# Attention numerators with tokens on partitions: q's exponentials become the stationary operand, the division happens on PSUM, and a TensorE transpose brings the result to x

## The chip, the cores and the metric

The kernel runs on one core of a Trainium2 chip. The metric is the device time of one execution in microseconds (us). The kernel before takes 989.12 us (median of three runs, 987.18 to 989.40). The execution that was profiled took 986.97 us, of which the profile's span is 984.9 us.

## The reference, cut to what matters

Linear attention with an exponential feature map, then two MLPs, one after the other:

```python
def phi(x):                                   # q, k, v: (4, 8, 576, 64) f32
    proj = einsum('bhsd,df->bhsf', x, w_phi)  # 128 features
    proj = proj - max(abs(proj), axis=-1)
    return concatenate([exp(proj), exp(-proj)], axis=-1)
q_p, k_p = phi(q), phi(k)
kv  = einsum('bhsf,bhsd->bhfd', k_p, v)
z   = sum(k_p, axis=2)
num = einsum('bhsf,bhfd->bhsd', q_p, kv)
den = einsum('bhsf,bhf->bhs', q_p, z)[..., None] + 1e-06
x   = (num / den) -> (2304 tokens, 512)
x   = elu(x @ w1_in) @ w1_out                 # 512 -> 2048 -> 512
out = h * clip(h + 3, 0, 6) / 6 @ w2_out      # h = x @ w2_in
```

The four MLP weights come as 64-bit floats. The kernel turns them into 32-bit floats with integer operations on the chip.

## The kernel before, in words

**Units.** The attention part is cut into 8 units. A unit is two heads of two batches, with 576 tokens each, laid as 9 tiles of 128 rows (64 tokens of one batch and 64 of the other). For each unit:

- `proj` (L316): TensorE projects k and q into four PSUM banks of ring "p".
- `peak` (L326) and `shift` (L340): VectorE takes the largest absolute value per row from PSUM and subtracts it. A unit has 8 such pairs 512 wide and 2 pairs 256 wide.
- `k_exp` (L349, L356): ScalarE makes k's exponentials of both signs.
- `kv` (L378): TensorE sums k's exponentials times [v, 1] into two banks, with 64 rows by 64 columns of the array in each matmul. Four places of the array are used in turn.
- `stat` (L393, L397): ScalarE copies these sums to SBUF (tile st). The sum z is repeated over the 64 columns that hold no values, so that the stationary operand is 128 columns wide.
- `q_tr`, `q_tr8` (L402, L408): TensorE transposes q's shifted projections into a bank of ring "t" (two banks). `q_exp` (L415, L424): ScalarE makes q's exponentials (tile e, features on partitions).
- `num` (L436): with st stationary (128 by 128) and e moving (256 or 320 tokens), 16 matmuls per unit make numerators on 64 partitions and the denominator, repeated, on the other 64. An f32 matmul leaves two records in the trace.
- `num_out` (L451, L455): ScalarE copies both to SBUF, with epsilon added to the denominators.
- `den`, `recip`, `recip_rows` (L460, L466, L474): VectorE transposes blocks of 32 by 32 so that each denominator is taken once, inverts, and transposes back. This happens four times per unit.
- `scale` (L483): GpSimd multiplies and writes x, with features on partitions, as the MLPs read it.

**Weights.** Each of the 64 weight tiles is converted by eight VectorE instructions (`begin` L681, `ts` L689, `into_b` L693) and then `end`, `w_hi`, `w_lo` on GpSimd (L698, L720, L726). A weight is held as a high and a low part, and so is x (`x_hi` on ScalarE L732, `x_lo` on VectorE L737).

**MLPs.** `hid` (L752) and `outp` (L813) each multiply three pairs of parts. Weights go in groups of four hidden tiles over all five blocks of tokens. The first block (512 tokens of batch 0) needs units 0 to 3 only, so its `hid` can start before the last unit is done.

**Order.** Nothing is ordered by hand. Each step has an engine, a planned duration, what it waits for, the buffers it takes and a rank. `in_order` plans all steps on all engines and the instructions are issued in the planned order, so every engine runs its own list strictly in turn. Ranks come from the unit's number times `PERIOD`, the length of the chain behind the step, and a table `BIAS` by kind of step. `W_LEAD` and `W_BIAS` rank the weight conversions.

Of the kernel before, what the change touches and what calls it, by code (L numbers as in the profile page):

```python
# [29 lines left out]
}  # L30
KVT = 0.118
W_LEAD, W_BIAS = 21.4, 113.0
# [19 lines left out]
WINDOW = 0.2  # L52
# [94 lines left out]
def attention_then_two_mlps(  # L147
# [82 lines left out]
    eps_c = bpool.tile([128, 1], F32, name="eps_c")  # L230
    nc.gpsimd.memset(eps_c, EPS)
# [7 lines left out]
    for i in range(2):  # L239
        t = apool.tile([128, R, 2, D + 1], F32, name=f"vb{i}")  # L240
        nc.gpsimd.memset(t[:, :, 0, D:D + 1], 1.0)
        nc.gpsimd.memset(t[:, :, 1, 0:1], 1.0)
        vb.append(t)
# [3 lines left out]
        "st0": 2, "st1": 2, "nsd": NSB, "t1": 1, "rr": 2, "rb": 2,  # L247
# [3 lines left out]
    MU = {}  # L251
    last = {}

    def unit(u):
# [12 lines left out]
        raw, P, M, SH, KP, acc, E, ST, NS, RB = ({} for _ in range(10))  # L267
# [10 lines left out]
        def load_v():  # L278
            src = v[u].rearrange("p (r h d) -> p r h d", r=R, h=2)
            for h in range(2):  # L280
                nc.sync.dma_start(out=vb[u % 2][:, :, h, h:h + D], in_=src[:, :, h])
# [102 lines left out]
        def stat_at(h):  # L384

            return (slice(0, 65), slice(64, 65), slice(65, 128)) if h == 0 else (
                slice(63, 128), slice(63, 64), slice(0, 63)
            )

        def stat(h):  # L390
            st = ST[h] = bpool.tile([128, 4, 128], F32, tag=f"st{h}", name="st", bufs=2)
            for bb in range(2):
                nc.scalar.copy(  # L393
                    out=st.rearrange("p (e b) d -> p e b d", e=2)[:, :, bb, stat_at(h)[0]], in_=acc[bb][:, h]
                )
            _, z, c = stat_at(h)
            nc.scalar.copy(out=st[:, :, c], in_=st[:, :, z].to_broadcast([128, 4, 63]))  # L397
# [13 lines left out]
        def q_exp(h, c):  # L411
            e = E[h, c] = bpool.tile([128, 2, 2, 4 + c, 64], F32, tag="e", name="e", bufs=EB)
            ps = P.pop(("q", h, c)).rearrange("p (r b t) -> p r b t", r=4, b=2)
            for half in range(2):
                nc.scalar.activation(  # L415
                    out=e[:, half, :, 0:4, :].rearrange("p b r t -> p r b t"), in_=ps, func=AF.Exp,
                    scale=1.0 if half == 0 else -1.0,
                )

        def q_exp8():  # L420
            ps = P.pop(("q", 8))
            for h in range(2):
                for half in range(2):
                    nc.scalar.activation(  # L424
                        out=E[h, 1][:, half, :, 4, :],
                        in_=ps[:, h * 128:(h + 1) * 128].rearrange("p (b t) -> p b t", b=2),
# [3 lines left out]
        def num(h, c, bb):  # L430
            e = E[h, c].rearrange("p e b r t -> p (e b r t)")
            n = 64 * (4 + c)
            ps = bank("t")
            for half in range(2):
                o = (half * 2 + bb) * n
                nc.tensor.matmul(  # L436
                    out=ps[:, :n], lhsT=ST[h][:, half * 2 + bb, :], rhs=e[:, o:o + n],
                    start=(half == 0), stop=(half == 1),
                )
            P["n", h, c, bb] = ps  # L440

        def num_out(h, c, bb):
            n = 64 * (4 + c)
            ps = P.pop(("n", h, c, bb))
            if (c, bb) not in NS:
                NS[c, bb] = tuple(
                    bpool.tile([128, 320], F32, tag="n" + s_, name="n" + s_, bufs=NSB) for s_ in "sd"
                )
# [565 lines left out]
```

## Time and profile before

| | before |
|---|---|
| median of three runs | 989.12 us (987.18 to 989.40) |
| the profiled execution | 986.97 us, span 984.9 us |
| TensorE (PE) busy | 966.0 us, 98% |
| VectorE (DVE) busy | 743.8 us, 76% |
| ScalarE (ACT) busy | 422.6 us, 43% |
| GpSimd (POOL) busy | 276.9 us, 28% |

The shares are means over two very different stages: the attention part, up to about 180 us, and the MLPs behind it. They have to be read apart. A busy PE is not PE at its peak: the ends of matmuls are modelled, and neighbours overlap.

### The profile page before, as it was taken

Reading aid. Unit: us, or ns where it says so; the run is one execution under the profiler, and the core shown is the slowest. Engines: PE = TensorE matmul, PEld = TensorE weight load, DVE = VectorE, ACT = ScalarE, POOL = GpSimd, SP = SyncE. Lnnn points to the kernel's source line nnn. Section 1 sums busy time; section 2 is a strip of 40 time slices with the busy share of each in tenths; the row PEclk is TensorE's granted clock in tenths of the full one; section 3 lists DMA queues with packets and bytes.
Section 4 is the critical chain, followed back from the end, with each engine's and each line's share of the span. In section 5 each row is a group of like instructions: output and inputs, shape, how many; then the busy total and the mean of one; then the engine's idle time right before and its main releaser. Section 6 shows DMA issues by size and latency. Waiting matters only on the chain.

```text
span 984.9 us, 17242 instructions
## 1 busy us (share of the span) xinstructions
PE 966.0 (98%) x7040; PEld 803.2 (82%) x7040; DVE 743.8 (76%) x1222; ACT 422.6 (43%) x831; POOL 276.9 (28%) x256
## 2 busy tenths in 40 slices
PE   8999999999999999999999999999999999999998
PEld 7777777788888888888887888888888888888887
DVE  5999999999858956895698958955986599643333
ACT  4888788864353333333344443333222222222222
POOL 0122323334234213421355363313321333130000
PEclk9999999999999999999999999999999999999999
DMA  7343321012202110211011201220122012001111
GB/s 210 107 133 107 96 79 38 23 44 65 84 2 65 55 53 1 65 52 56 1 44 43 65 22 44 65 65 1 44 65 65 1 43 65 22 1 43 43 43 64
DMA packets 33310, 53.66 MB, mean 54 GB/s; under 512 B 20304, under 2 KB 20432, under 8 KB 33232
## 3 DMA queue, kind: packets, MB, share of 16 engines
q1 hardware_dynamic: 33232, 52.57, 17.6%
q8 instruction: 55, 0.90, 0.4%
q14 instruction: 23, 0.19, 0.1%
HBM read 47.84 MB, written 4.72 MB: 53 GB/s over the span
## 4 chain that ended last, share of the span: by engine, by line
PE 81%; DVE 14%; ACT 4%; issue 1%; DVEq 0%; POOL 0%; ACTq 0%; POOLq 0%
PE ps_p L752 39%; PE ps_a L813 20%; PE ps_t L813 18%; DVE mx L326 3%; DVE shq L340 2%; PE ps_p L316 1%; DVE shk L340 1%; DVE w_b L693 1%; DVE rb L474 1%; DVE t L460 1%; DVE w_a L689 1%; DVE gl L794 1%; PE ps_t L436 1%; ACT kp L349 1%; ACT e L415 1%
## 5 line engine op out<-in xcount | busy, mean ns | idle before, releaser
L779 DVE SCALAR_TENSOR_TENSOR g<-e,ps_p 128x512 f32<-128x512 f32 (+1 forms) x160 | 101.1, 632 | 161.6 <-ACT e L768 105.9
L752 PE MATMUL ps_p<-xh,w_l 128*128 128x512 f32 (+1 forms) x512 | 185.6, 362 | 0.0
L752 PE MATMUL ps_p<-xl,w_h 128*128 128x512 f32 (+1 forms) x512 | 185.6, 362 | 0.0
L752 PE MATMUL ps_p<-xh,w_h 128*128 128x512 f32 (+1 forms) x512 | 185.5, 362 | 0.0
L698 POOL TENSOR_TENSOR w_b<-w_b,w 128x512 int32<-128x512 int32 x64 | 91.4, 1428 | 303.3 <-DVE w L689 303.3
L794 DVE TENSOR_TENSOR gl<-g,gh 128x512 fp32r<-128x512 f32 (+1 forms) x160 | 123.6, 773 | 47.9 <-ACT gh L787 43.7
L768 ACT ACTIVATE e<-ps_p,half_c 128x512 f32<-128x512 f32 (+1 forms) x80 | 51.7, 646 | 224.0 <-PE ps_p L752 224.0
L787 ACT CAST gh<-g 128x512 fp32r<-128x512 f32 (+1 forms) x160 | 92.6, 578 | 119.3 <-DVE g L779 119.2
L765 ACT ACTIVATE e<-ps_p 128x512 f32<-128x512 f32 (+1 forms) x80 | 44.4, 555 | 168.6 <-PE ps_p L752 168.6
L752 PEld LDWEIGHTS ps_p<-xh,w_h 128*128 128x128 f32 x512 | 96.6, 189 | 15.9
L752 PEld LDWEIGHTS ps_p<-xl,w_h 128*128 128x128 f32 x512 | 96.6, 189 | 15.9
L752 PEld LDWEIGHTS ps_p<-xh,w_l 128*128 128x128 f32 x512 | 96.5, 189 | 15.0
L689 DVE TENSOR_SCALAR w_a<-w_a 128x512 int32<-128x512 int32 x128 | 104.1, 813 | 1.4
L693 DVE SCALAR_TENSOR_TENSOR w_b<-w,w_b 128x512 int32<-128x512 int32 x128 | 89.6, 700 | 2.4
L726 POOL TENSOR_TENSOR w_l<-w_b,w_h 128x512 fp32r<-128x512 f32 x64 | 86.1, 1345 | 5.3
L720 POOL TENSOR_SCALAR w_h<-w_b 128x512 fp32r<-128x512 f32 x64 | 46.5, 726 | 139.4 <-PE ps_a L813 74.9
L436 PE MATMUL ps_t<-e,st 128*128 128x256 f32 (+1 forms) x256 | 70.4, 418 | 3.9 <-ACT st L397 2.8
L483 POOL TENSOR_TENSOR x<-ns,rb 128x256 f32<-128x256 f32 (+1 forms) x32 | 26.9, 842 | 140.1 <-DVE rb L474 95.7
L436 PEld LDWEIGHTS ps_t<-e,st 128*128 128x128 f32 x256 | 45.6, 189 | 21.5 <-ACT ns L455 7.0
L813 PE MATMUL ps_a<-w_h,gh 128*128 128x512 f32 x160 | 62.6, 391 | 0.1
L813 PE MATMUL ps_a<-w_h,gl 128*128 128x512 f32 x160 | 62.5, 391 | 0.0
L813 PE MATMUL ps_a<-w_l,gh 128*128 128x512 f32 x160 | 62.4, 390 | 0.0
(89 smaller groups left out, 1916.6 us busy)
## 6 DMA issues: line engine op xcount, KB each, us to landing
w<-in_moe_w_in_dram SPq DMA_DIRECT2D x32, 512.0 KB, 3.6
w<-in_moe_w_out_dram SPq DMA_DIRECT2D x32, 512.0 KB, 3.6
vb<-in_v_dram SPq DMA_DIRECT2D x16, 288.0 KB, 4.4
out_dram<-x SPq DMA_DIRECT2D x18, 256.0 KB, 2.1
raw_k<-in_k_dram SPq DMA_DIRECT2D x7, 576.0 KB, 6.1
raw_q<-in_q_dram SPq DMA_DIRECT2D x7, 576.0 KB, 3.8
raw_k<-in_k_dram SPq DMA_DIRECT2D x1, 320.0 KB, 5.1
raw_q<-in_q_dram SPq DMA_DIRECT2D x1, 320.0 KB, 5.5
```

The costliest lines, as they stand in the source:

```text
L436: nc.tensor.matmul(out=ps[:, :n], lhsT=ST[h][:, half * 2 + bb, :], rhs=e[:, o:o + n], start=(half == 0), stop=(half == 1),)
L689: V.tensor_scalar(out=st[o], in0=st[x], scalar1=s1, scalar2=s2, op0=o1, **kw)
L693: return lambda: V.scalar_tensor_tensor(out=st["b"], in0=st[x], scalar=s1, in1=st["b"], op0=o1, op1=ALU.bitwise_or)
L698: nc.gpsimd.tensor_tensor(out=st["b"], in0=st["b"], in1=st["l"], op=ALU.add)
L720: nc.gpsimd.tensor_scalar(out=W[w][0][:, i], in0=F[w, i], scalar1=1.0, scalar2=0.0, op0=ALU.mult, op1=ALU.add)
L726: nc.gpsimd.tensor_tensor(out=lo[:, i], in0=F.pop((w, i)), in1=hi[:, i].bitcast(F32), op=ALU.subtract)
L752: nc.tensor.matmul(out=ps[:, :n], lhsT=a_[:, 0, c], rhs=x_[kk], start=(i == 0), stop=(i == 3 * KD - 1),)
L768: nc.scalar.activation(out=e[:, :n], in_=ps[:, :n], func=AF.Relu, scale=1.0 / 6.0, bias=half_c)
L779: V.scalar_tensor_tensor(out=gt[:, :n], in0=e[:, :n], scalar=s, in1=ps[:, :n], op0=o0, op1=o1)
L787: nc.scalar.copy(out=gh[:, :n], in_=G[m, b, f][:, :n])
L794: V.tensor_tensor(out=gl[:, :n], in0=gt[:, :n], in1=gh[:, :n].bitcast(F32), op=ALU.subtract)
L813: nc.tensor.matmul(out=o, lhsT=a_, rhs=b_, start=(fi == 0 and i == 0), stop=(fi == fn - 1 and i == 2))
```

## The change

Numerators are now made with tokens on the partitions. For every tile of 128 rows, head and sign, q's exponentials are the stationary operand, 64 columns for one batch and 64 for the other, and [kv, z] of that batch (65 columns) is the moving one. That is 72 matmuls per unit in three chunks of three tiles, where 16 wide ones were. The 65th column is the denominator of the row. VectorE adds epsilon, inverts six values per row and multiplies straight out of PSUM; TensorE transposes the quotient (9 transposes per unit), and ScalarE copies it to x. The block transposes on VectorE, the copies `num_out`, the widening of st and the multiplication on GpSimd are gone. The planner's tables have other numbers.

```diff
-KB, QB, KPB, EB, NSB, MXB, WB, GB = 3, 6, 3, 4, 2, 6, 4, 2
-PERIOD, PROJ, TURN = 27.5, 0.22, 0.19
+KB, QB, KPB, EB, NRB, MXB, WB, GB = 3, 6, 3, 4, 2, 6, 4, 2
+PERIOD, PROJ, TURN = 21.5, 0.22, 0.19
 BIAS = {
...
-W_LEAD, W_BIAS = 21.4, 113.0
+W_LEAD, W_BIAS = -24.8, 143.2
...
-        def stat(h):
-            st = ST[h] = bpool.tile([128, 4, 128], F32, tag=f"st{h}", name="st", bufs=2)
+        def stat():
+            st = ST[0] = bpool.tile([128, 2, 2, 2, D + 1], F32, tag="st", name="st", bufs=2)
             for bb in range(2):
...
-            _, z, c = stat_at(h)
-            nc.scalar.copy(out=st[:, :, c], in_=st[:, :, z].to_broadcast([128, 4, 63]))
+                nc.scalar.copy(out=st[:, bb], in_=acc[bb])
...
-        def num(h, c, bb):
-            e = E[h, c].rearrange("p e b r t -> p (e b r t)")
-            n = 64 * (4 + c)
+        def num(ch):
+
+            ps = bank("t", (128, 3, 2, D + 1))
+            for i in range(3):
+                r = 3 * ch + i
+                c = int(r >= 4)
+                for h in range(2):
+                    for half in range(2):
+                        for bb in range(2):
+                            p = slice(64 * bb, 64 * bb + 64)
+                            nc.tensor.matmul(
+                                out=ps[p, i, h], lhsT=E[h, c][:, half, r - 4 * c, p],
+                                rhs=ST[0][:, bb, h, half], start=(half == 0), stop=(half == 1),
+                            )
+            P["n", ch] = ps
+
+        def den(ch):
+            dn = DN[ch] = bpool.tile([128, 3, 2], F32, tag="dn", name="dn", bufs=2)
+            V.tensor_scalar(out=dn, in0=P["n", ch][:, :, :, D], scalar1=EPS, scalar2=None, op0=ALU.add)
+            V.reciprocal(out=dn, in_=dn)
+
+        def scale(ch):
+            nr = NR[ch] = bpool.tile([128, 3, 2, D], F32, tag="nr", name="nr", bufs=NRB)
+            V.tensor_tensor(
+                out=nr, in0=P.pop(("n", ch))[:, :, :, 0:D],
+                in1=DN.pop(ch).unsqueeze(3).to_broadcast([128, 3, 2, D]), op=ALU.mult,
+            )
+
+        def x_tr(ch):
             ps = bank("t")
...
+            nr = NR.pop(ch).rearrange("p i h d -> p i (h d)")
+            for i in range(3):
+                nc.tensor.transpose(ps[:, i * 128:(i + 1) * 128], nr[:, i], ident)
+            P["x", ch] = ps
+
+        def x_out(ch):
+            nc.scalar.copy(
...
+                in_=P.pop(("x", ch))[:, :384].rearrange("p (r b t) -> p r b t", r=3, b=2),
             )
```

The removed bodies of `num_out`, `den`, `recip`, `recip_rows` and `scale` stand in the listing above.

**VectorE in the middle of a unit.** Before (mx, sh: projections; w, w_a, w_b: weight conversion; t, rr, rb: block transposes of denominators):

```order
L693 SCALAR_TENSOR_TENSOR w_b<-w_a,w_b 128x512
L460 STREAM_TRANSPOSE t_1710<-nd 128x256
L466 RECIPROCAL rr<-t_1710 128x8
L474 STREAM_TRANSPOSE rb<-rr 128x256
L689 TENSOR_SCALAR w_1012<-w_1012 128x512
L681 TENSOR_SCALAR w_a<-w_1402 128x512
L689 TENSOR_SCALAR w_a<-w_a 128x512
L460 STREAM_TRANSPOSE t_1755<-nd 128x256
L466 RECIPROCAL rr<-t_1755 128x8
```

And the same place now (dn: inverted denominators, nr: quotients):

```order
L651 SCALAR_TENSOR_TENSOR w_b<-w_a,w_b 128x512
L433 TENSOR_SCALAR dn<-ps_t_1659 128x6
L434 RECIPROCAL dn<-dn 128x6
L438 TENSOR_TENSOR nr<-ps_t_1659,dn 128x384
L647 TENSOR_SCALAR w_955<-w_955 128x512
L639 TENSOR_SCALAR w_a<-w_1306 128x512
L323 TENSOR_REDUCE mx<-ps_p_1690 128x4
L337 TENSOR_TENSOR shk<-ps_p_1690,mx 128x512
```

The first chunk's three small steps read the PSUM bank itself. Three more pairs of the next unit's k stand between them and the second chunk's.

**TensorE, the numerators of one unit.** Before (st, e: as above; ps_t: a bank of ring "t"):

```order
L316 MATMUL ps_p_2127<-wphi,raw_q 128x128
L436 MATMUL ps_t_2151<-e,st 128x320 x2
L436 MATMUL ps_t_2164<-e,st 128x320 x2
L436 MATMUL ps_t_2181<-e,st 128x320 x2
L436 MATMUL ps_t_2188<-e,st 128x320 x2
L402 MATMUL ps_t_2203<-ident,shq 128x128 x4
```

And now the second and third chunk:

```order
L313 MATMUL ps_p_2117<-wphi,raw_k 128x128
L447 MATMUL ps_t_2136<-ident,nr 128x128 x3
L389 MATMUL ps_t_2144<-ident,shq 128x128 x4
L395 MATMUL ps_t_2155<-ident,sh_1652 128x128 x2
L425 MATMUL ps_t_2168<-st,e 64x65 x24
L425 MATMUL ps_t_2202<-st,e 64x65 x24
L447 MATMUL ps_t_2240<-ident,nr 128x128 x3
```

Transposes of quotients, transposes of q and numerators now take turns in the two banks of ring "t", so a bank of one must be read before the next may be written.

**VectorE where the MLPs begin.** Before, the last pair of q (mx, shq) stands ahead of the last low part of x for the first block (x0q, x0k):

```order
L474 STREAM_TRANSPOSE rb<-rr 128x320
L737 TENSOR_TENSOR x0q_2933<-x_74,x0q_2932 128x512
L326 TENSOR_REDUCE mx<-ps_p_2891 128x4
L340 TENSOR_TENSOR shq<-ps_p_2891,mx 128x512
L737 TENSOR_TENSOR x0q_2933<-x_74,x0k_2930 128x512
```

Now:

```order
L695 TENSOR_TENSOR x0k_3175<-x_74,x0k_3174 128x512
L337 TENSOR_TENSOR shq<-ps_p_3116,mx 128x512
L695 TENSOR_TENSOR x0k_3175<-x_74,x0q_3176 128x512
L695 TENSOR_TENSOR x0q_3177<-x_74,x0q_3176 128x512
L695 TENSOR_TENSOR x0q_3177<-x_74,x0k_3174 128x512
L323 TENSOR_REDUCE mx<-ps_p_3117 128x4
L337 TENSOR_TENSOR shq<-ps_p_3117,mx 128x512
```

The low parts of x now come ahead of the last three of the last unit's pairs of q (one of the three is shown). Seven weight conversions have begun by then, before and now.

## Rows read from the trace of the kernel before

**Rows 1.** The chain that ended last, from the page: share of the span by engine.
```profile
PE 81%; DVE 14%; ACT 4%; issue 1%; DVEq 0%; POOL 0%; ACTq 0%; POOLq 0%
```

**Rows 2.** Busy time by stage: stretch, length, busy us of each engine, clock, DMA.
```profile
20.00:180.00 160.00, 151.34 (x2961) 119.96 (x2963) 151.58 (x287) 134.99 (x323) 42.65 (x46) 0.99 0.31 95
180.00:200.00 20.00, 19.77 (x113) 15.28 (x105) 19.48 (x33) 16.33 (x36) 7.95 (x7) 1.00 0.09 28
200.00:985.00 785.00, 779.53 (x3697) 654.27 (x3695) 563.89 (x891) 264.57 (x462) 225.40 (x192) 1.00 0.14 44
```

**Rows 3.** ScalarE in order of time, st copies of units 0 and 6: start, us, what.
```profile
26.91 0.44 ACT L393 COPY st<-ps_a 128x130 f32<-128x130 f32 x2 [0.77 <-PE ps_a L378]
...
159.46 0.46 ACT L393 COPY st<-ps_a 128x130 f32<-128x130 f32 x2
```

**Rows 4.** VectorE's groups from 20 to 180 us: busy us, mean ns of one, idle before.
```profile
L326 DVE TENSOR_REDUCE mx<-ps_p 128x4 f32<-128x512 f32 x57 | 38.5, 675 | 0.0
L340 DVE TENSOR_TENSOR shq<-ps_p,mx 128x512 f32<-128x512 f32 x30 | 20.2, 674 | 0.6
...
L689 DVE TENSOR_SCALAR w_a<-w_a 128x512 int32<-128x512 int32 x14 | 11.0, 788 | 0.2
L693 DVE SCALAR_TENSOR_TENSOR w_b<-w,w_b 128x512 int32<-128x512 int32 x12 | 8.2, 687 | 0.2
L474 DVE STREAM_TRANSPOSE rb<-rr 128x320 f32<-128x320 f32 x14 | 7.2, 512 | 1.8 <-DVE rr L466 0.5
L689 DVE TENSOR_SCALAR w_b<-w 128x512 int32<-128x512 int32 x7 | 7.0, 996 | 0.0
L460 DVE STREAM_TRANSPOSE t<-nd 128x320 f32<-128x320 f32 x14 | 7.0, 497 | 0.0
L340 DVE TENSOR_TENSOR sh<-ps_p,mx 128x256 f32<-128x256 f32 x16 | 6.8, 425 | 0.5
...
L474 DVE STREAM_TRANSPOSE rb<-rr 128x256 f32<-128x256 f32 x14 | 6.2, 446 | 1.3
L460 DVE STREAM_TRANSPOSE t<-nd 128x256 f32<-128x256 f32 x14 | 6.1, 437 | 1.4 <-ACT nd L451 1.4
L681 DVE TENSOR_SCALAR w_a<-w 128x512 int32<-128x512 int32 x7 | 5.5, 791 | 0.0
...
L466 DVE RECIPROCAL rr<-t 128x8 f32<-128x8 f32 x14 | 2.9, 204 | 0.5
```

**Rows 5.** VectorE in order of time.
```profile
154.74 1.09 DVE L689 TENSOR_SCALAR w_b<-w 128x512 int32<-128x512 int32 x1
...
178.97 0.68 DVE L737 TENSOR_TENSOR x0q<-x,x0k 128x512 fp32r<-128x512 f32 x1
...
179.90 0.42 DVE L689 TENSOR_SCALAR w_b<-w 128x512 int32<-128x512 int32 x1
```

**Rows 6.** GpSimd in order of time.
```profile
154.65 0.89 POOL L483 TENSOR_TENSOR x<-ns,rb 128x320 f32<-128x320 f32 x1 [1.44 <-DVE rb L474]
```

**Rows 7.** TensorE in order of time, unit 5, and the first hidden-layer matmul.
```profile
133.33 1.09 PE L402 MATMUL ps_t<-ident,shq 128*128 128x128 f32 x8
134.36 2.56 PE L378 MATMUL ps_a<-vb,kp 64*64 64x65 f32 x160
...
138.15 1.99 PE L436 MATMUL ps_t<-e,st 128*128 128x256 f32 x8
...
145.08 4.82 PE L436 MATMUL ps_t<-e,st 128*128 128x320 f32 x16
...
180.38 0.73 PE L752 MATMUL ps_p<-x0k,w_h 128*128 128x512 f32 x2
```

**Rows 8.** TensorE's weight loads, 20 to 180 us, by group.
```profile
L436 PEld LDWEIGHTS ps_t<-e,st 128*128 128x128 f32 x224 | 39.8, 189 | 18.9 <-ACT ns L455 5.8 <-ACT st L397 3.9
L378 PEld LDWEIGHTS ps_a<-vb,kp 64*64 64x64 f32 x2099 | 33.1, 134 | 5.5 <-issue 5.1 <-DMA w<-in_moe_w_in_dram 0.2 <-DMA w<-in_moe_w_out_dram 0.2
```

**Rows 9.** ScalarE's groups, 20 to 180 us.
```profile
L415 ACT ACTIVATE e<-ps_t 128x512 f32<-128x512 f32 x61 | 32.5, 602 | 21.5 <-PE ps_t L402 21.3
```

More of the change, by code (lines that the diff above doesn't have):

```diff
@@ L265, in add @@
             return s
-        raw, P, M, SH, KP, acc, E, ST, NS, RB = ({} for _ in range(10))
+        raw, P, M, SH, KP, acc, E, ST, DN, NR = ({} for _ in range(10))
         Tk = {}
@@ L442, in num_out @@
[L442 to L448, printed above, removed]
-            ns, ds = NS[c, bb]
-            p0, z0 = 64 * h, 64 - 64 * h
-            nc.scalar.activation(
-                out=ds[p0:p0 + 64, :n], in_=ps[z0:z0 + 64, :n], func=AF.Identity,
-                bias=eps_c[z0:z0 + 64], scale=1.0,
-            )
-            nc.scalar.copy(out=ns[p0:p0 + 64, :n], in_=ps[p0:p0 + 64, :n])
@@ L527, in unit @@
                     S_[f"KV{j}{h}"].behind.append(S_["KVk00"])
-        for h in range(2):
-            t = Tk["st", h] = take(f"st{h}")
-            add(f"ST{h}", "ACT", 0.8, bind_(stat, h), after=[f"KV{j}{h}" for j in ("k0", "k1", "x8")],
-                takes=[t], uses=[Tk["acc", 0], Tk["acc", 1]], stage="ST")
+        Tk["st"] = take("st")
+        add("ST", "ACT", 0.75, stat, after=[f"KV{j}{h}" for j in ("k0", "k1", "x8") for h in range(2)],
+            takes=[Tk["st"]], uses=[Tk["acc", 0], Tk["acc", 1]], stage="ST")
         for c in range(2):
@@ new lines, in unit @@
+        for ch in range(3):
+            t, td, tn, tx = take("t"), take("dn"), take("nr"), take("t")
+            cs = [[0], [0, 1], [1]][ch]
+            add(f"NM{ch}", "PE", 12 * KVT, bind_(num, ch),
+                after=["ST"] + [f"QE{h}{c}" for h in range(2) for c in cs] + ["QE8"] * (ch == 2), takes=[t],
+                uses=[Tk["st"]] + [Tk["e", h, c] for h in range(2) for c in cs], stage="NM", rows=66)
+            add(f"RT{ch}", "DVE", 0.3, bind_(den, ch), after=[f"NM{ch}"], takes=[td], uses=[t])
+            add(f"RB{ch}", "DVE", dve(384), bind_(scale, ch), after=[f"RT{ch}"], takes=[tn], uses=[t, td])
+            add(f"XT{ch}", "PE", 3 * 0.109, bind_(x_tr, ch), after=[f"RB{ch}"], takes=[tx], uses=[tn], stage="XT")
+            XC[u, ch] = add(f"XC{ch}", "ACT", act(384), bind_(x_out, ch), after=[f"XT{ch}"], uses=[tx])
+            if ch:
+                S_[f"NM{ch}"].behind.append(S_[f"NM{ch - 1}"])
+                S_[f"XT{ch}"].behind.append(S_[f"XT{ch - 1}"])
@@ L859, in attention_then_two_mlps @@
             chain = x
-            cost = [0.34, 0.34, 0.34, 0.34, 0.62, 0.62, 0.62, 0.34]
+            cost = [0.31, 0.31, 0.31, 0.46, 0.62, 0.62, 0.62, 0.31]
             fns = to_f32(w, i)
@@ L878, in covers @@
         return [
-            s for (u, c, bb), s in MU.items()
-            if u % KD == kk and (a := (2 * (u // KD) + bb) * S + 256 * c) < t0 + n and a + 64 * (4 + c) > t0
+            s for (u, ch), s in XC.items()
+            if u % KD == kk and any(
+                (a := (2 * (u // KD) + bb) * S + 192 * ch) < t0 + n and a + 192 > t0 for bb in range(2)
+            )
         ]
```

94 lines of the change are left out of this document (14 added, 80 removed), and 6 rows, old and new, of the table BIAS.

## The prediction

> **What bounds the kernel now.** I read the chain of waits first: by engine, 81% of it is TensorE and 14% VectorE [rows 1]. That is a mean over stages, so I read the busy time by stage next [rows 2]. From 200 us on, TensorE is busy 779.53 of 785 us while VectorE has 28% left: there only TensorE's own work counts. From 20 to 180 us VectorE is busy 151.58 of 160 us, TensorE 151.34 and ScalarE 134.99. Nearly every VectorE group of that stage shows no idle time ahead of it [rows 4]. TensorE's 95% there is stretched by overlapping records, so VectorE is what paces the attention part, with TensorE close behind. The copies of st for units 0 and 6 are 132.55 us apart [rows 3], so one unit takes 22.09 us. The first hidden-layer matmul starts at 180.38 us [rows 7], 0.7 us after VectorE ends the last low part of x for the first block (178.97 plus 0.68, [rows 5]). So the time is: how long VectorE takes to get there, then TensorE's remaining work.
>
> **The change part by part.**
>
> VectorE, removed per unit: two rounds on 256 columns and two on 320, each a block transpose, a reciprocal and a block transpose back. That is 2 x (0.437 + 0.204 + 0.446) + 2 x (0.497 + 0.204 + 0.512) = 4.60 us [rows 4].
>
> VectorE, added per unit: three chunks. The addition of epsilon and the reciprocal have six values per row. I price each as the reciprocal of eight, 0.204. The product reads 384 values from PSUM against a repeated operand, as `shift` does; it lies between shift's 256 (0.425) and 512 (0.674) [rows 4], and I take the middle, 0.55. Sum 3 x 0.96 = 2.87, so VectorE gains 1.73 us per unit; the bounds of the product make it 1.36 to 2.10.
>
> VectorE, freed by GpSimd: the same conversion step takes 1.09 us when GpSimd's multiplication runs beside it (154.65 to 155.54, [rows 6]) and 0.42 us when nothing does [rows 5]. In the attention part the mean is 0.996 for w_b, 0.788 for the two on w_a and 0.791 for L681 [rows 4]. If all four fell to 0.42, the unit would gain 0.58 + 2 x 0.37 + 0.37 = 1.69 us; if none did, nothing. The multiplications leave GpSimd altogether, while its three weight steps remain. The order puts two of the four behind three pairs of k, where those should be over. I take 1.2, near the upper end.
>
> TensorE per unit. Now: 151.34 / 160 x 22.09 = 20.9 us busy [rows 2]. Removed: 16 records in 4.80 (145.08 to 149.88) and twice 8 in 1.93, 8.66 us [rows 7]. Added: 72 matmuls, that is 144 records, with all 128 rows and 64 columns of the array. No row shows that shape. The nearest is `kv`: 160 records of 65 columns in 2.56 us, 16 ns each, with four places of the array taking turns [rows 7]. If all four run at once, a record takes 64 ns at its place, and two places give 32 ns. If only places with different rows run at once, a record takes 32 ns, and the new ones, one after another, again 32. So I expect 144 x 0.032 = 4.6, and 0.1 for each chunk's start: 4.9 us. The upper end is four at once in `kv` and none here, 144 x 0.064 = 9.2, 9.5 with the starts; the lower end is `kv`'s own 16 ns, 2.4 us with nothing gained by it, since TensorE has room. Added too: nine transposes at 1.09 / 8 = 0.136, 1.2 us [rows 7]. Sum 20.9 - 8.66 + 4.9 + 1.2 = 18.3 us. TensorE drops further below VectorE, so its gain is cover, not time.
>
> A rule speaks against these 4.9 us. Loads of weights lie under matmuls in this trace: from 200 us on both are busy at once, 779.53 and 654.27 of 785 us, with the same 128 rows in every load and every matmul [rows 2]. The Trainium skill, "TensorE: Matmul & The Clock Gate", Part 3 (The mechanism), says that a load overlaps matmuls in flight only when its group of rows differs. By it the new numerators, which all use the same rows, would show every load; these rows disagree with it, and what it would cost is the fourth rival.
>
> ScalarE loses 16 copies (`num_out`) and the widening of st and gains three copies of 384 per unit. It is not the bound now and will be less so; I count nothing. If it hid a delay, this would be in the loop below.
>
> Waits added. The two banks of ring "t" tie the engines in a loop. Between the first chunk's product and the second chunk's addition VectorE has two conversion steps (0.42 to 0.8 each) and three pairs (3 x 1.35): 4.9 to 5.6 us. In that time the quotient must be transposed (3 x 0.136), then q (4 x 0.136), ScalarE must make two exponentials of 0.602 [rows 9], and TensorE the second chunk (1.6): 3.8 us, plus five hand-overs between engines. That leaves 1.1 to 1.8 us for the hand-overs, so VectorE will sometimes stand at the addition, and everything behind it on VectorE's list (the other pairs, the conversions) stands with it. A second such place is the first chunk, behind the pairs of q. No row prices this; below is 0, above is 2.5 us per unit (both places late by a whole chunk of 1.6, less the slack). I take 1.0.
>
> Per unit: 22.09 - 1.73 - 1.2 + 1.0 = 20.16 us, 1.93 less. Seven units' numerators stand ahead of the first hidden-layer matmul, before and after: -13.5 us. Order around it: three pairs of q move behind the last low part of x (3 x 1.35 = 4.05 us less ahead of it), and two more 0.42 steps and one of 0.687 stand ahead of it: -2.5. They are hidden then under the first hidden-layer matmuls. The first of these starts near 164.4 us.
>
> After it, TensorE had 8.66 us of numerators left. Now it has 14 transposes of q (1.9), 72 matmuls (4.9) and 9 transposes (1.2), 8.0 us: -0.7. The MLPs themselves have the same matmuls; seven weight conversions have begun by then in either order. I count nothing for them.
>
> Sum: -13.5 - 2.5 - 0.7 = -16.7 us. Against the profiled execution's 986.97 that is 970.3. The median of the runs shown is 2.15 above that execution, and the profiled one lies just below all three; I add 1 and forecast 971 us.
>
> **The rivals.**
>
> 1. The loop is the bound. VectorE waits 2.5 us per unit instead of 1.0: +10.5 over seven units, 981.5. For it: only two banks in ring "t", now with three kinds of users whose readers sit on two engines, and engines that run their lists strictly in turn. Against it: on paper the loop closes with a microsecond left.
>
> 2. VectorE gets all of it. No waits and the full 1.69: 7 x (1.0 + 0.49) = 10.4 less, 961. For it: in the trace of before VectorE stands at almost no group [rows 4]. Against it: TensorE at 18.3 plus its own waits comes close to the 18.7 us that VectorE would need.
>
> 3. The halves run one after the other (slower). If matmuls with all rows and 64 columns do not run side by side, numerators cost 9.5 us per unit, TensorE needs 18.3 + 4.6 = 22.9, with 0.5 of waits for exponentials 23.4, against 22.09 now: +9.2 over seven units, -2.5 for the order, and behind the first hidden-layer matmul 1.9 + 9.5 + 1.2 - 8.66 = +3.9. Sum +10.6, 998. It decides from about 47 ns per record on, where TensorE reaches VectorE's 20.16. For it: no row shows this shape. Against it: it needs `kv`'s places to run four at once, those with common rows among them, and two with common rows not to do so here [rows 7].
>
> 4. As 3, and each load shows as well. A load of 128 columns takes 0.189 and one of 64 takes 0.134 [rows 8], so 64 columns are worth 0.055. Then 144 x 0.119 = 17.1, with the starts 17.4 us: TensorE 30.8 per unit, +61; behind the first hidden-layer matmul +11.8; order -2.5; 1058. Against it: the overlap in rows 2.
> That is what the rule of the Trainium skill above (same page, same section) would give, and the trace disagrees with it wherever it shows loads.
>
> 5. The weights come late. The table now ranks conversions later. If the MLPs wait for the eighth tile by about one conversion of eight steps (some 5 us), 976. Against it: the same number has begun by the first hidden-layer matmul.
>
> **How the numbers follow.** The forecast 0.50, with its own range 964 to 977 (product 1.36 to 2.10, relief 0 to 1.69 and waits of 0 to 2.5 not all at one end). Rival 1 0.22, rival 2 0.10, rival 3 0.11, rival 4 0.02, rival 5 0.05. The range 959 to 985 holds the forecast, rivals 1 and 5 and most of 2, and leaves out rivals 3 and 4. This kernel's three runs lie within 0.2%, so a difference below 0.2% (2 us) is no change that can be told. Faster: the forecast, rivals 2 and 5 and nearly all of rival 1, 0.84. Same: the far end of rival 1 and the near end of rival 3, 0.04. Slower: rivals 3 and 4, 0.12.
>
> **What the profile of the changed kernel would show.** Copies of st 20 us apart, not 22. The 48 records of a chunk in about 1.6 us; 3.1 would be rival 3, more rival 4. The w_b step near 0.42 in the attention part. Idle time on VectorE ahead of the addition of epsilon, released by TensorE: 1 us per unit, and 2.5 if rival 1 holds. The first hidden-layer matmul near 164 us, and from there as much time to the end as now. The forecast is wrong if TensorE has no gaps in the attention part, if its granted clock, 0.99 from 20 to 180 us now [rows 2], drops in that stage because gaps become longer, or if it waits behind the first hidden-layer matmul for weights.

## The result and the profile after

The changed kernel takes 973.02 us (median of four runs, 970.64 to 975.75) against 988.66 us for the kernel before (four runs, 987.18 to 989.40). The ratio is 0.9849, 95% interval 0.9833 to 0.9865, so it is faster by 15.6 us. The forecast was 971 us.

| | before | after |
|---|---|---|
| profiled execution, span | 986.97, 984.9 us | 975.75, 973.8 us |
| first hidden-layer matmul | 180.38 us | 171.99 us |
| from there to the end of the span | 804.5 us | 801.8 us |
| TensorE busy | 966.0 us | 944.7 us |
| VectorE busy | 743.8 us | 707.8 us |
| ScalarE busy | 422.6 us | 367.2 us |

The profiled execution happens to be the slowest of the four. From its page: TensorE's busy time, the queue that brings instructions (packets, MB, share), and the chain of waits by engine, against [rows 1]:

```profile
PE 944.7 (97%) x8008; PEld 800.4 (82%) x8008; DVE 707.8 (73%) x1198; ACT 367.2 (38%) x695; POOL 251.5 (26%) x221
...
q8 instruction: 63, 1.03, 0.4%
...
PE 93%; ACT 3%; issue 2%; DVE 2%; POOL 0%; POOLq 0%; DVEq 0%; ACTq 0%
```

VectorE's share fell from 14% to 2%. TensorE now holds the chain to the end, and issue, time in which an engine waited for nothing that the profile shows, rose from 1% to 2%. Busy time by stage, against [rows 2] (stretch, length, busy us of PE, PEld, DVE, ACT, POOL, granted clock, DMA share, GB/s):

```profile
20.00:180.00 160.00, 141.86 (x3873) 125.08 (x3868) 134.49 (x273) 88.53 (x206) 23.06 (x21) 0.96 0.33 95
180.00:200.00 20.00, 19.65 (x180) 15.95 (x176) 17.08 (x36) 12.66 (x27) 3.33 (x3) 1.00 0.10 35
200.00:974.00 774.00, 769.62 (x3659) 647.34 (x3657) 547.46 (x878) 259.21 (x453) 224.26 (x188) 1.00 0.13 43
...
120.00:127.70 7.70, 5.37 (x233) 4.94 (x231) 5.73 (x9) 1.41 (x3) 0.00 (x0) 1.00 0.26 81
127.80:134.40 6.60, 6.54 (x72) 5.54 (x74) 2.23 (x6) 4.00 (x10) 0.00 (x0) 0.50 0.41 92
```

In the attention part no engine is full any more: TensorE has 18 us without work in 160, VectorE 25. The granted clock fell from 0.99 to 0.96. The last two rows show one of the falls, from 2.4 to 1.2 GHz (1.00 to 0.50). VectorE's groups, against [rows 4]:

```profile
L438 DVE TENSOR_TENSOR nr<-ps_t,dn 128x384 f32<-128x384 f32 x21 | 11.7, 558 | 0.8
...
L323 DVE TENSOR_REDUCE mx<-ps_p 128x2 f32<-128x256 f32 x16 | 6.7, 420 | 11.6 <-PE ps_p L313 11.6
L647 DVE TENSOR_SCALAR w_a<-w_a 128x512 int32<-128x512 int32 x14 | 5.9, 423 | 0.2
...
L434 DVE RECIPROCAL dn<-dn 128x6 f32<-128x6 f32 x21 | 4.0, 192 | 0.7
L639 DVE TENSOR_SCALAR w_a<-w 128x512 int32<-128x512 int32 x8 | 3.6, 450 | 0.0
L433 DVE TENSOR_SCALAR dn<-ps_t 128x6 f32<-128x6 f32 x21 | 3.3, 157 | 2.1 <-PE ps_t L425 2.0
L647 DVE TENSOR_SCALAR w_b<-w 128x512 int32<-128x512 int32 x7 | 2.9, 421 | 0.0
```

The three new steps take 0.157, 0.192 and 0.558 us. The integer steps have fallen to 0.42 to 0.45. VectorE hardly stands at the addition of epsilon (2.0 us in all). It stands at the peaks, above all those of tile 8, the ninth and last tile of a unit, whose peaks are 256 wide (11.6 us). The waits from 20 to 180 us (who for whom, us in all, times, the longest):

```profile
DVE mx L323 <- PE ps_p L313: 15.2, 8, 5.2
...
PE ps_a L375 <- issue: 11.1, 7, 2.5
...
DVE dn L433 <- PE ps_t L425: 2.0, 3, 1.0
```

TensorE in order of time shows how the first two hang together:

```profile
99.01 3.49 PE L375 MATMUL ps_a<-vb,kp 64*64 64x65 f32 x223
104.99 0.21 PE L375 MATMUL ps_a<-vb,kp 64*64 64x65 f32 x1 [2.49 <-issue]
105.13 1.09 PE L389 MATMUL ps_t<-ident,shq 128*128 128x128 f32 x8
106.16 0.49 PE L313 MATMUL ps_p<-wphi,raw_k 64*128 64x128 f32 x4
...
107.94 1.62 PE L425 MATMUL ps_t<-st,e 128*64 128x65 f32 x48 [0.33 <-ACT e L402]
...
116.68 0.52 PE L447 MATMUL ps_t<-ident,nr 128*128 128x128 f32 x3
...
122.23 3.14 PE L375 MATMUL ps_a<-vb,kp 64*64 64x65 f32 x198
127.86 1.13 PE L375 MATMUL ps_a<-vb,kp 64*64 64x65 f32 x26 [2.49 <-issue]
128.91 1.97 PE L389 MATMUL ps_t<-ident,shq 128*128 128x128 f32 x8
```

Numerators take 1.62 us per chunk of 48 records, as forecast. But kv, which stood in runs of 160, 64 and 64 records before, now has a run of 224, five of a unit's six steps. TensorE stands 2.5 us in the middle of it, between two records of the same step. The projection of tile 8 (L313, raw_k, x4) is queued behind that run, and VectorE waits for it. After the second stand eight transposes take 1.97 us in place of 1.09: that is the stretch at the lower clock above (0.50, from 127.80 us).

### The profile page after: what moved, and what is told of

Same layout as the page of the kernel before. It is cut to its first block, busy times and chain, and to the rows that moved or that the text cites. A ratio compares the mean times of both kernels' runs of the same rounds, so it can differ in the third digit from the quotient of the medians.

```text
span 973.8 us, 18895 instructions
## 1 busy us (share of the span) xinstructions
PE 944.7 (97%) x8008; PEld 800.4 (82%) x8008; DVE 707.8 (73%) x1198; ACT 367.2 (38%) x695; POOL 251.5 (26%) x221
## 3 DMA queue, kind: packets, MB, share of 16 engines
q8 instruction: 63, 1.03, 0.4%
## 4 chain that ended last, share of the span: by engine, by line
PE 93%; ACT 3%; issue 2%; DVE 2%; POOL 0%; POOLq 0%; DVEq 0%; ACTq 0%
PE ps_p L710 40%; PE ps_a L771 21%; PE ps_t L771 19%; PE ps_a L375 4%; PE ps_t L425 4%; PE ps_p L313 3%; ACT e L402 2%; PE ps_t L447 1%; PE ps_t L389 1%; PE ps_t L233 0%; ACT x L451 0%; DVE gl L752 0%; DVE xl L695 0%; ACT st L384 0%; DVE g L737 0%
## 5 line engine op out<-in xcount | busy, mean ns | idle before, releaser
L752 DVE TENSOR_TENSOR gl<-g,gh 128x512 fp32r<-128x512 f32 (+1 forms) x160 | 118.8, 743 | 53.7 <-ACT gh L745 48.9
L647 DVE TENSOR_SCALAR w_a<-w_a 128x512 int32<-128x512 int32 x128 | 99.1, 774 | 2.0
L323 DVE TENSOR_REDUCE mx<-ps_p 128x4 f32<-128x512 f32 (+1 forms) x80 | 50.4, 630 | 26.2 <-PE ps_p L313 26.2
L771 PE MATMUL ps_a<-gl,w_h 128*128 128x512 f32 (+1 forms) x160 | 59.3, 370 | 0.2
L771 PE MATMUL ps_a<-gh,w_h 128*128 128x512 f32 (+1 forms) x160 | 59.0, 369 | 0.0
```

What stands on the lines that cost most here:

```text
L323: V.tensor_reduce(out=mx[:, :n], in_=P[j, h], axis=AX.X, op=ALU.max, apply_absolute_value=True)
L647: V.tensor_scalar(out=st[o], in0=st[x], scalar1=s1, scalar2=s2, op0=o1, **kw)
L752: V.tensor_tensor(out=gl[:, :n], in0=gt[:, :n], in1=gh[:, :n].bitcast(F32), op=ALU.subtract)
L771: nc.tensor.matmul(out=o, lhsT=a_, rhs=b_, start=(fi == 0 and i == 0), stop=(fi == fn - 1 and i == 2))
```

## The experiments

Theory 1: TensorE runs out of instructions in kv. Each record is two instructions (weight load and matmul) every 16 ns, and the page's row of the instruction queue shows 63 packets with 1.03 MB, for TensorE's 8008 loads and 8008 matmuls: 64 bytes each, and 16 KB or some 256 instructions, 128 records, per packet. Theory 2: kv waits for data (k's exponentials, its banks, v). Theory 3: the loads' traffic delays it. Theory 4: VectorE's and TensorE's work paces the stage, and the stands are left over.

Every kernel is compared with runs of the kernel before on the same chip, and kernels with each other by these ratios.

**control**: the changed kernel again, nothing edited. 

> The changed kernel itself, on the chip of the next three. Every theory expects 971 to 976 us, with VectorE standing about 26 us in all at the 256-wide peaks and TensorE standing some 14 us in the middle of kv.

972.88 us, ratio 0.9838 [0.9822, 0.9855]. Its profiled execution (969.67) has less of the lower clock: granted 0.99 from 20 to 180 us, first hidden-layer matmul at 165.69. kv stands 8.4 us and VectorE 10.7 us at the peaks, from 20 to 180 us. (Over the whole span these are 11.4 and 21.0, a little less than the 14 and 26 that were expected; the changed kernel's first profiled execution has 14.5 and 26.2.)

**kv_wide**: half as many instructions in kv.

```diff
-                    for f0 in (0, 64):
-                        for bb in range(2):
...
-                                out=acc[bb][f0:f0 + 64, h, half], lhsT=kp[p, i, half, f0:f0 + 64],
+                    for bb in range(2):
...
+                            out=acc[bb][:, h, half], lhsT=kp[p, i, half, :],
```

> kv with 128 stationary columns per matmul in place of 64: 72 matmuls per unit where 144 were, the same sums, the same order. If TensorE stands in the middle of kv because it runs out of instructions (theory 1), half as many bytes of them in kv bring the 14 us of standing below 5 us, VectorE's 26 us at the peaks of tile 8 to about 11 us as before the change, and the time to about 963 us (seven units, 1.5 us each less). If kv stands because of something it waits for (k's exponentials, the two banks, the load of v; theory 2), over 10 us of standing remain and the time stays within 2 us of the control. If two places of 128 columns carry less than four of 64 (some 60 ns per record as in proj, in place of two times 16), kv takes 4 us more per unit and the time goes above 980 us.

981.2 us, ratio 0.9949 [0.9925, 0.9973]. TensorE in order of time:

```profile
68.26 6.37 PE L374 MATMUL ps_a<-vb,kp 64*128 64x65 f32 x112
```

No stand of a kv matmul for issue is left, but a record takes 57 ns (6.37 / 112), so the run takes 6.37 us where 224 records at 16 ns take 3.5. (The row is from an execution of 991.36 us, at full clock in this stretch.) The third case came: two places of 128 columns carry less than four of 64. As a test of theory 1 it is weak, since slower records alone would also give the fetch time.

**tile8_first**: the last three steps of kv moved by hand behind the next unit's projection of tile 8.

```diff
+        late = [NAMED[u, n] for n in ("KVk11", "KVx80", "KVx81")]
...
+        at = planned.index(NAMED[u + 1, "PJx8"]) + 1
+        planned[at:at] = late
```

> The same instructions; in each unit the projection of tile 8 of the next unit (4 matmuls) moves ahead of the last three steps of kv, so kv's run of 224 records becomes one of 128 and one of 96. Theory 1: the bytes are the same, so TensorE still stands over 8 us in all in kv, but VectorE's wait at the 256-wide peaks falls from 26 to under 13 us, and the time falls by 5 to 10 us against the control (963 to 968). Theory 4 (TensorE's work and gaps pace the stage, VectorE's standing is only what is left over): VectorE stands elsewhere instead, and the time stays within 2 us.

988.4 us, ratio 1.0006 [0.9996, 1.0016]. The test is void, through my edit: the steps were moved past the copies of st, which then lack their sums, and past the load of v into the buffer that they read. kv stands 19.5 us for v, and VectorE 30.0 us at the additions. It says nothing on the theories. kv_split below asks the same by a rule of the planner.

**gpsimd_back**: GpSimd multiplies again.

```diff
+            junk = bpool.tile([128, 384], F32, tag="junk", name="junk", bufs=1)
+            nc.gpsimd.tensor_tensor(
+                out=junk, in0=nr.rearrange("p i h d -> p (i h d)"), in1=nr.rearrange("p i h d -> p (i h d)"),
+                op=ALU.mult,
+            )
```

> GpSimd multiplies again: after each chunk's product it makes one more 128 by 384 product into a tile that nobody reads (the same 1152 columns per unit as before the change), everything else as in the changed kernel. If GpSimd's product slows VectorE's integer steps beside it, as I took it in the prediction (1.2 us per unit of relief, at most 1.69), w_a and w_b rise from 0.42 to 0.7 to 1.0 us and the time rises by 6 to 12 us against the control (979 to 985). If VectorE's standing at the peaks covers it (3 us per unit), the steps rise all the same but the time rises by less than 3 us.

974.95 us, ratio 0.9866 [0.9848, 0.9884]: 2.1 us above the control, with overlapping intervals. From 20 to 180 us the steps on w_a read (L645 and L653 are L639 and L647 of the control):

```profile
L653 DVE TENSOR_SCALAR w_a<-w_a 128x512 int32<-128x512 int32 x14 | 8.5, 605 | 0.2
L645 DVE TENSOR_SCALAR w_a<-w 128x512 int32<-128x512 int32 x8 | 6.1, 757 | 0.0
L653 DVE TENSOR_SCALAR w_b<-w 128x512 int32<-128x512 int32 x7 | 2.9, 419 | 0.0
```

Three of the four steps rise beside GpSimd (0.42 to 0.61 twice, 0.45 to 0.76), 0.67 us per unit. Taken one by one, the integer steps that overlap nothing on GpSimd take 0.42 us (18 of them), those beside the product alone 0.59 on average (11), and those beside the product and a weight step 0.97 (6), so the contention is shown. In the time it shows as some 2 us, less than the 4.7 us of seven units. That fits the second case, in which VectorE's standing covers the rest.

**kv_alone**: kv's matmuls on constant data, with nothing to wait for.

> No attention and no MLPs, only four stretches of matmuls on constant data, nothing to wait for inside a stretch: 1024 matmuls as in kv (64 rows by 64 columns, 2048 records), 512 as in the numerators (128 by 64, 1024 records), 256 as in the wide kv (64 by 128, 512 records), then 2048 more as in kv (4096 records) while loads of k and q run. Theory 1 (instructions run out): the first stretch stands every 128 records (256 instructions of weight load and matmul) once what was fetched ahead is used up, for 1 to 2.5 us each time, so 128 records take 3.5 to 4.5 us in the steady state and not 2.05; numerators at 31.5 ns (4.0 us per 128) stand little or not at all, and the wide ones at 62 ns not at all. Theory 2 (kv waits for data): 16 ns per record throughout. Theory 3 (the loads' traffic delays TensorE): no standing in the first stretch, standing in the fourth.

TensorE in order of time (start, us, what, idle before):

```profile
1.24 7.42 PE L212 MATMUL ps_a<-vb,kp 64*64 64x65 f32 x351 [1.24 <-POOL vb L197]
10.24 2.09 PE L212 MATMUL ps_a<-vb,kp 64*64 64x65 f32 x128 [1.58 <-issue]
14.24 2.09 PE L212 MATMUL ps_a<-vb,kp 64*64 64x65 f32 x128 [1.91 <-issue]
...
56.08 2.09 PE L212 MATMUL ps_a<-vb,kp 64*64 64x65 f32 x128 [1.91 <-issue]
...
63.81 27.83 PE L223 MATMUL ps_c<-vb,kp 128*64 128x65 f32 x929 [0.36 <-issue]
91.57 28.36 PE L212 MATMUL ps_d<-vb,kp 64*128 64x65 f32 x504
...
139.05 3.57 PE L212 MATMUL ps_b<-vb,kp 64*64 64x65 f32 x128 [2.91 <-issue]
...
156.98 2.09 PE L212 MATMUL ps_b<-vb,kp 64*64 64x65 f32 x128 [1.64 <-issue]
```

After the first 351 records TensorE stands every 128 records exactly, 1.4 to 1.9 us each time. From 10.24 to 56.08 us there are twelve such rounds, 3.82 us each, of which 2.09 are work. Numerators (30.0 ns per record) and wide matmuls (56.3 ns) run on without a stand, but for one of 0.36 us. So the supply is one piece of 256 instructions in 3.8 us, and whatever uses them faster must stand. Theory 2 falls. While the loads ran, up to about 148 us and partly at the lower clock, the rounds took 5.1 to 6.2 us (127.75, 132.85, 139.05, 144.42). So loads lengthen the rounds, but the stands are there without them, and theory 3 is not their cause.

The kept trace also holds the times of the instruction queue's packets, and they show theory 1 directly. Packets of 16384 bytes land at 12.75, 16.57 and 20.53 us, and kv's records begin again at 14.24, 17.97 and 21.98. In each of the 14 stands of the first stretch TensorE goes on 1.2 to 1.5 us after a packet has landed, and the next packet sets out 1.0 to 1.7 us after that. These two delays and the packet's own 0.9 to 1.4 us make up the round. The control has the same: packets land at 100.34, 121.65, 143.14 and 162.56, and kv goes on at 101.64, 123.14, 144.53 and 163.96.

**shift_64**: the place of the pieces moved by 64 records.

```diff
-    WARM = 16
+    WARM = 16 + 64
```

> 64 more dummy transposes on TensorE at the very start, in the time in which it waits for the first load; nothing else changed. In the control, kv's run of 224 records is broken after 223, 198, 172 and 147 records in units 4, 5, 6 and 7 (25 or 26 less each time). Theory 1 (the break is at a multiple of 256 instructions of TensorE's list): with 64 records (128 instructions) more ahead, it moves to 159, 134, 108 (or 236) and 83 (or 211) in the same units, and stands longest where it is late in the run. Theory 2 or 3 (data, banks, loads): the breaks stay where they were, 223, 198, 172, 147.

The broken runs of the control's units 4 to 7, in order of time:

```profile
101.64 0.21 PE L375 MATMUL ps_a<-vb,kp 64*64 64x65 f32 x1 [1.91 <-issue]
123.14 0.68 PE L375 MATMUL ps_a<-vb,kp 64*64 64x65 f32 x26 [2.22 <-issue]
144.53 1.03 PE L375 MATMUL ps_a<-vb,kp 64*64 64x65 f32 x52 [1.33 <-issue]
163.96 1.39 PE L375 MATMUL ps_a<-vb,kp 64*64 64x65 f32 x77 [0.49 <-issue]
```

and those of shift_64:

```profile
112.11 1.17 PE L375 MATMUL ps_a<-vb,kp 64*64 64x65 f32 x65 [0.84 <-issue]
131.34 1.61 PE L375 MATMUL ps_a<-vb,kp 64*64 64x65 f32 x90 [0.37 <-issue]
153.59 0.37 PE L313 MATMUL ps_p<-wphi,raw_k 64*128 64x128 f32 x1 [0.22 <-issue]
172.69 0.45 PE L375 MATMUL ps_a<-vb,kp 64*64 64x65 f32 x13 [1.43 <-issue]
```

The last number of a row is what was left of the run. 224 less 65, 90 and 13 gives breaks after 159, 134 and 211 records in units 4, 5 and 7, as theory 1 said to the record. In unit 6 the break moved out of kv into the projection behind it, 235 records after kv's start (236 was the second case named). The break follows the count of instructions and not the data. It also explains why it walks by 25 or 26 records per unit, and why it costs most where it comes late in the run, when kv has used up what was ahead. (977.03 us is a single run.)

**kv_split**: the planner gets one more rule, and kv stands in runs of 64 and 80 records.

```diff
+        if u > 1:
+            NAMED[u - 1, "KVk11"].behind.append(S_["PJx8"])
```

> The same instructions, planned again with one more rule: the projection of tile 8 of the next unit must start before the last-but-one big step of kv. In the steady state kv's matmuls now stand in runs of 32 and 40 (64 and 80 records) with the slower projections, transposes and a copy's wait between them, where there was a run of 112 (224 records). Theory 1: kv's standing for issue falls from 8.4 us to under 3 us and VectorE's wait at the 256-wide peaks from 21 to under 6 us; the time falls by 7 to 10 us against the control, to 963 to 966. Theory 2: the standing stays above 7 us and the time within 3 us of 973. Theory 4 (VectorE and TensorE pace the stage at about 20 us per unit whatever kv does): the standing goes and as much comes back elsewhere, 971 to 975.

970.41 us, ratio 0.9817 [0.98, 0.9834]. The waits from 20 to 180 us:

```profile
DVE mx L326 <- PE ps_p L316: 6.9, 1, 6.9
...
PE ps_a L378 <- issue: 1.0, 2, 0.6
```

kv's stand for issue is down to 1.0 us, as theory 1 said. VectorE stands 6.9 us at the peaks, once (13.2 over the whole span, as the expectation counted, where theory 1 had under 6). But the time fell by 2.5 us only, not 7 to 10, with overlapping intervals, and the first hidden-layer matmul came at 166.26. In this order TensorE waits for exponentials (4.8), for q's shifts (3.3), for copies of x out of the two banks (2.1) and for quotients (1.8), and VectorE for numerators (4.6, in the control 1.6). Still, up to the first hidden-layer matmul VectorE stands 4.5 us less than in the control (24.35 against 28.80). It is busy 5.0 us more (141.91 against 136.89): the new plan put more conversion steps ahead of that matmul, and the first step, L644, takes 0.854 us on average where it took 0.455. So theory 1 is right on the cause, and the time came out nearer to theory 4's, but not by waits alone: this run doesn't price the stand.

**old_tables**: the new numerators with the planner's numbers of before.

```diff
-PERIOD, PROJ, TURN = 21.5, 0.22, 0.19
+PERIOD, PROJ, TURN = 27.5, 0.22, 0.19
...
-W_LEAD, W_BIAS = -24.8, 143.2
+W_LEAD, W_BIAS = 21.4, 113.0
```

> The new numerators with the planner's numbers of before (those that it still has; the two new kinds of step keep theirs). kv then stands in runs of 80 and 128 or 144 records, all three chunks of numerators in one run, and the weights begin earlier. If the gain is the numerators' own (VectorE's 1.7 us per unit and the relief), the time stays within 4 us of the control, 969 to 977. If the order that the new numbers give is what closes the loop of the two banks, VectorE stands about 2 us per unit at the additions of epsilon, and the time is 985 or more.

966.74 us, ratio 0.9788 [0.9772, 0.9803]: faster than the changed kernel, and below both cases of the expectation. From 20 to 180 us kv's longest run is 128 records and it stands 4.4 us; VectorE stands 2.9 us at the peaks and 2.3 at the additions. The profiled execution (962.11 us) has no lower clock in the attention part, and its first hidden-layer matmul is at 158.20. So by the ratios the numerators are worth about 21 us, and the new PERIOD, BIAS, W_LEAD and W_BIAS give 5 to 6 of them back. The 21 include what else the change altered in the planner and this run keeps: WINDOW (0.2 to 0.3), the planned lengths of the conversion steps, and that all eight steps of a conversion, not six, are now planned apart from GpSimd's work.

**old_tables_gpsimd**: the two edits together. 

> The new numerators with the planner's numbers of before, and GpSimd's product of 128 by 384 after each chunk's product again (into a tile that nobody reads). With these numbers VectorE stood only some 8 us in all from 20 to 180 us, so what its integer steps lose beside GpSimd should show in the time. If the steps lose as much as with the new numbers (0.18 us on each of the two on w_a, 0.31 on the first: 0.7 us per unit): 4 to 5 us above old_tables, 970 to 972. If they fall beside GpSimd in full as they did before the change (1.7 us per unit): 978. If VectorE does not pace the stage even here: within 2 us of 966.7.

969.21 us, ratio 0.9789 [0.9766, 0.9813], the same as old_tables. But here the step on w_a stayed at 0.423: of 36 integer steps only one fell beside GpSimd's products. So it prices no contention, only GpSimd's work as such, at nothing.

**replanned**: a third set of numbers. 

> The changed kernel with a third set of the planner's numbers, picked so that, with the durations of these traces and one chunk of 256 TensorE instructions every 3.73 us, the list comes out short: kv stands in runs of 96, 32 and 16 with transposes and projections between, all three chunks of numerators in one run. The durations give a first hidden-layer matmul near 155 us where the same reckoning gives 170 for the control (measured 165.7) and 166 for old_tables (measured 159.7), so I expect 952 to 962 us, below old_tables (966.7). If the reckoning misses what paces the stage, it lands between old_tables and the control, 966 to 973.

967.35 us, ratio 0.9772 [0.9748, 0.9796]: not to be told from old_tables, and short of the 952 to 962 that my reckoning gave. kv still stands 8.2 us, up to 3.1 at once, and the clock is at 0.96 from 20 to 165 us. Its first hidden-layer matmul came at 165.01, not near 155. (For old_tables the trace has 158.20, where the expectation says 159.7.) A supply of one piece per 3.73 us, taken as steady, was too kind: in kv_alone the rounds took 5.1 to 6.2 us while loads ran.

**vector_back** and **old_tables_vector**: VectorE gets back about what the change took off it.

```diff
+            junk = bpool.tile([128, 384], F32, tag="junk", name="junk", bufs=1)
+            V.transpose(out=junk, in_=nr.rearrange("p i h d -> p (i h d)"))
```

> The changed kernel with one more block transpose of 128 by 384 on VectorE after each chunk's product, into a tile that nobody reads: some 0.56 us each, 1.7 per unit, what the change took off VectorE. If VectorE paces the attention part (the prediction's step), seven units give +12 us against the control (985). If TensorE's standing and the wait behind it at the peaks pace it, VectorE has 1.5 us per unit there to give: +1 to 4 us (974 to 977).

> The same three block transposes with the planner's numbers of before. There VectorE stood only 8 us in all from 20 to 180 us, so if it paces that order, +8 to 12 us against old_tables (975 to 979); if TensorE does (busy 126.5 of 135 us there), +2 to 5 us (969 to 972).

A transpose took 0.578 us, so 1.73 per unit and 12.1 us over seven units. vector_back takes 979.01 us, ratio 0.9913 [0.9898, 0.9928], 0.76% above the control: 7.4 us. old_tables_vector takes 973.39 us, ratio 0.9859 [0.9844, 0.9874], 0.73% above old_tables: 7.1 us. Both lie between the two cases. About 60% of the work that VectorE got back shows in the time; the rest fits into time in which it stood.

## Why the prediction was right, and which terms were off

**VectorE's own work.** What was removed was 4.60 us per unit; what was added is 3 x (0.157 + 0.192 + 0.558) = 2.72, where I had 2.87. The product at 0.558 is the middle that I took. In the changed kernel VectorE sets the pace of the attention part only partly: by vector_back, 60% of the work put back shows in the time.

**The numerators on TensorE.** 48 records in 1.62 us, with 30 ns from one start to the next; three transposes in 0.52 to 0.55. This is the forecast's 1.6. Rival 3 (64 ns) and rival 4 (119 ns) are out, and kv_alone gives 30.0 ns by itself. The rule of the Trainium skill that I weighed ("TensorE: Matmul & The Clock Gate", Part 3, The mechanism) would, taken by itself, have shown every load; the trace disagrees with it.

**The relief.** I took 1.2 us per unit, at most 1.69. It came nearly in full: 0.996 to 0.421 on w_b, 0.788 to 0.423 twice, 0.791 to 0.450, together 1.65 [rows 4]. This step was undersized by 0.45. Its reason, that the multiplications leave GpSimd, holds only in part. In the trace of before, the integer steps from 20 to 180 us spend 12.2 us above 0.42 each: 4.6 beside the multiplication alone, 2.7 beside it and the weight step L698, and 4.9 beside L698 alone, which is still there after the change. And with the product put back, in gpsimd_back, 0.67 of the 1.65 came back. The rest came with the new order, in which 29 of 36 of these steps overlap nothing on GpSimd (2 of 34 before).

**The waits: the step that failed.** "VectorE will sometimes stand at the addition", 1.0 us per unit. The loop of the two banks closed: 2.0 us in all, 0.3 per unit, so rival 1 did not happen. In its place came a wait that I had not looked for: at the peaks, behind kv's run, 15.2 us in the stage of the profiled execution, 2.2 per unit (10.7 in the control, 1.5). I had read the order at VectorE's additions and at the numerators, but not that kv's three runs became two and one of them 224 records long. I also gave kv's 16 ns per record to any length of run; beyond what is fetched ahead it is 3.8 us per 128, 30 ns (kv_alone).

The sum with measured terms: 22.09 - 1.88 - 1.65 + 0.3 + 2.2 = 21.1 us per unit for the profiled execution and 20.3 for the control (0.2 and 1.5). The copies of st, against [rows 3], give 20.6 and 19.9, some 0.4 less. The forecast overlooked that VectorE stood before too, 1.21 us per unit between these copies (125.31 of 132.55 us busy) and part of it at the block transposes that are gone:

```profile
27.41 0.73 ACT L384 COPY st<-ps_a 128x260 f32<-128x260 f32 x2
...
171.68 0.65 ACT L384 COPY st<-ps_a 128x260 f32<-128x260 f32 x2 [2.99 <-PE ps_a L375]
```

(That is 144.27 us over seven units; the control's first and last are at 26.03 and 165.37. The forecast was 20.16.) Two errors of opposite sign, relief too small and waits in another place, nearly cancel. The forecast of 971 was right in part by luck of that kind.

The count that needs no unit is VectorE's time up to the first hidden-layer matmul, before and in the control:

```profile
0.00:180.38 180.38, 167.10 (x3264) 133.96 (x3265) 160.75 (x301) 142.10 (x335) 43.58 (x58) 0.98 0.35 105
...
0.00:165.69 165.69, 143.47 (x4098) 126.64 (x4098) 136.89 (x277) 89.45 (x206) 20.59 (x27) 0.99 0.40 115
```

Its busy time fell by 23.9 us, and its idle time rose by 9.2 us, where the forecast has 7.0 (in the profiled execution after the change 23.2 and 14.8). Of the work, counted step by step up to the start of the next, the block transposes, inversions and quotients gave 11.0 us (28.3 to 17.3; forecast 7 x 1.73 = 12.1), the conversions 12.4 (36.3 to 24.0; forecast 7 x 1.2 = 8.4) and the order 1.2 (forecast 2.5). So the matmul came 14.7 us earlier in the control, not 16.0, by several errors that nearly cancel.

**The order at the first hidden-layer matmul** was to bring 2.5 us. On VectorE it did its part: the last low part of x ends at 170.47 (169.78 plus 0.69). But the matmul starts 1.5 us later and not 0.7: on TensorE's list it stands behind kv's last run, with its stand, and four transposes of q:

```profile
170.26 1.39 PE L375 MATMUL ps_a<-vb,kp 64*64 64x65 f32 x77 [0.77 <-issue]
171.58 0.66 PE L389 MATMUL ps_t<-ident,shq 128*128 128x128 f32 x4
171.99 0.71 PE L710 MATMUL ps_p<-x0k,w_h 128*128 128x512 f32 x2
```

In the control it is 1.3 us (165.69 against 164.43). So 0.5 to 0.8 us of this term were lost to TensorE's own list. In that time VectorE went on with the pairs that were to be hidden: when the matmul starts, 79 of 80 peaks and 78 of 80 shifts have begun in the control, where 77 of each were meant to stand ahead.

**The clock.** The text named as a sign against it a clock that drops because gaps become longer. In the profiled execution it dropped, from 0.99 to 0.96 from 20 to 180 us, and one of the stretches begins at the end of the 2.5 us stand before 127.86. In the control it stayed at 0.99. Runs of one kernel differ along with it: old_tables took 962.11 us at a mean granted clock of 1.000 and 969.61 at 0.993. The profiled execution's first hidden-layer matmul comes 6.3 us behind the control's (171.99 and 165.69; forecast 164.4). It has more of the lower clock, and kv stands longer in it (11.1 us against 8.4); what each costs was not separated.

**After the first hidden-layer matmul** I expected -0.7 us; it was -2.7 (801.8 against 804.5), -2.5 in the control (967.7 less 165.69). TensorE was busy 1.6 us less there (797.28 against 798.92) and idle 1.1 us less (4.53 against 5.60). Rival 5 did not happen: TensorE is busy 769.62 of 774 us from 200 us on and waits for no weights.

**What is open**: how the stands, the lower clock and the new waits share the 5 to 6 us between the two tables. kv_split shows that the stands can go and most of the time stay, but with more VectorE work in the same stretch. The kernel before was not run with the new numbers, so what they would do without the new numerators is not known.

## What to carry to other kernels

When a change replaces few wide instructions by many short ones, or lets short ones stand together, count the instructions per microsecond of each run, beside the work. Here another order of the same instructions, with runs of at most 128 records in place of 224, is 0.5% faster; how much of it by this is open. An idle time that begins in the middle of a step and is released by nothing is a hint that instructions run short; shift the list by half a piece and see whether it moves, or look when the instruction queue's packets land. And read the order on the engine that is waited for at every long run, not only at the places that the change touches.

## What the hardware showed that I had not expected

TensorE's instructions arrive in pieces of 256, and a steady stream of kv's records gets one piece in 3.8 us: a loss of 1.4 to 1.9 us at each boundary. The next packet sets out only after TensorE has gone on with the last one (1.0 to 1.7 us after, in kv_alone where no loads ran), which is why the round doesn't get shorter where TensorE is quicker. The Trainium skill, "Runtime: NRT & Kernel Launch", section "Instruction fetch mechanics", says that instructions are refilled in blocks of 256 and that crossing a boundary is mostly hidden. The trace agrees with the first and, for records of 16 ns, not with the second; at 30 ns and more it is hidden here too, but for one stand of 0.36 us.

A record of 65 moving columns takes 16.3 ns with four places of 64 by 64, 30.0 ns with two places of 128 rows and 64 columns, and 56.3 ns with two places of 64 rows and 128 columns. For the whole array, the wide numerators of before (256 columns in 1.99 us per 8 records, [rows 7]) give an estimate of 63 ns for 65 columns. So the two places with common rows do run side by side. For the two with 128 columns the number of moving columns is not what counts: the projections, in the same places, take 64 ns per record of 128 (32 records in 2.06 us in the control). What does limit them is open.
